# ScalarE's tanh in another order, and the 24-point transforms of later batches spread over four groups

## The chip, the cores and the metric

The kernel runs on one core of one Trainium2 chip. The metric is the device time of one execution in microseconds (us). Shorter is better. Engines are named TensorE (PE in the profile), VectorE (DVE), ScalarE (ACT), GpSimd (POOL) and SyncE (SP, which here only issues DMAs).

## The reference

Three parts follow each other on 24,576 tokens of 256 values (8 batches of 3072), all in float32:

```python
X = np.fft.fft(x, axis=1); X = np.fft.fft(X, axis=2); x = X.real      # part 1, x: (8, 3072, 256)
h = x @ w_in; x = (h - np.tanh(h)) @ w_out                            # part 2, w_in 256x2048, w_out 2048x256
logits = x @ w_gate                                                   # part 3, 8 experts
e = argmax(logits); g = softmax(logits)[e]
out[token] = g * (np.maximum(x @ w1[e], 0) @ w2[e])                   # w1 256x1024, w2 1024x256
```

## The kernel before

Phase 1 computes parts 1 and 2 and the gate for one group of 1024 tokens after the other: 24 groups g, three to a batch (c = g mod 3: first, second and third pass of a batch), and one short pass at the end. The token axis is transformed as 24 x 128: 24-point transforms on VectorE and GpSimd, ahead of time and a batch at once, and a 128-point stage as matmuls at the start of the group before the one that uses it (`dft`, tile `dps`). The transform along the 256 values is folded into w_in.

A group takes 18 steps f. At step f, `uv` makes two products U and V of feature tile f on TensorE (six matmuls of 512 columns: high times high, high times low, low times high part), VectorE reads U into `us` (line 414) and forms h = us - v and us + v (423, 424), one tile for each half of the tokens (s = 0, 1). `tanh` takes each h twice on ScalarE: `t`, in full float32 (432), and `hi`, rounded (433). One step later `split_lo` forms the low part lo = t - hi (440), on GpSimd for s = 0 and on VectorE for s = 1, and `tmm` multiplies hi (eight matmuls, 452) and lo (four, 456) of the step before with w_out into four accumulators. Steps 16 and 17 form the linear part of the output instead of a tanh. All engines work in the order in which the code is written.

In the same steps the gate of the group before is computed: logits (f2, f3), the maximum and softmax (f4 to f6), places within the experts (f7, `place`; its last instruction, line 545, turns them into whole numbers). From f8 to f15 GpSimd writes one column of rows a step to DRAM: a copy of gate and token (576) and an indirect DMA (568), the scatter.

The 24-point transform of a later batch nb is cut into single instructions by `fft_tasks`. Its first 24 steps, each one TENSOR_TENSOR of 128x768 on line 242, go to GpSimd (for batch 1 some to VectorE); the rest, on line 256, go to VectorE. `when` lists the steps of phase 1 that carry them. GpSimd has one of them in each of 24 steps of the third pass of batch nb - 2 (f0 to f14, then from f17 on) and in the first pass of batch nb - 1. VectorE has its part in steps 8 to 15 of that first pass and in 3 to 6 and 8 to 15 of the second. Each comes behind the step's other work on its engine. `load_x` brings the batch from DRAM, issued four steps before the first of them. Two buffers take turns: ya and yb.

Phase 2 is the experts' products. The change does not touch it. The lines on which the sums rest are these, in the order of one step:

```python
hl = [split_lo(th[0], G), split_lo(th[1], V)]     # G: GpSimd, V: VectorE
...
tmm(f - 1, hl)                                    # TensorE, behind the step's U and V
...
th = tanh(hs) if f < KF else None                 # ScalarE
```

Of the kernel before, what the change touches and what calls it, by code (L numbers as in the profile page):

```python
# [10 lines left out]
F32R = mybir.dt.float32r  # L11
# [15 lines left out]
# a row in DRAM: the low halves of its values, their high halves, gate and token, filled up  # L27
ROW = 272
# The rows of an expert come in a first block of 256, then in blocks of 512 and 256. With rows beyond
# the first 256 in pieces of 256, there are 88 to 95 pieces, and at least 40 pairs of one expert.  # L30
# [8 lines left out]
# 24-point classes: (k1 mod 8, k1 mod 3) -> k1; the other classes are mirror images  # L39
# [3 lines left out]
# row of a batch's buffer that holds the real and the sine part of class kb  # L43
# [11 lines left out]
def when(nb):  # L55
    """the steps of phase 1 that carry batch nb's transform: 24 on Pool, the others on DVE"""
    if nb == 1:
        steps = [t for t in range(12, 32) if t != 18]
        return [steps[i * 19 // 24] for i in range(24)], [32, 33, 34, *range(37, 41), *range(42, 50)]
    s = NSTEP * (NCH * nb - 4)  # L60
    return ([s + i + 2 * (i > 14) for i in range(24)],
            [t for t in range(s + 26, s + 52) if t % NSTEP not in (0, 1, 2, 7, 16, 17)])


def parts(kb, ka):
    """slots of a batch's buffer that hold the real and the sine part of class (kb, ka)"""
    if kb in (0, 4):
        return (ROWR[kb], 2 if ka else 0), ((ROWJ[kb], 1) if ka else None)
    return (ROWR[kb], ka), (ROWJ[kb], ka)
# [10 lines left out]
def shape_constants():  # L80
# [17 lines left out]
    # direct and mirrored columns (rows) to even and odd half (columns), for two columns at a time  # L98
# [6 lines left out]
    c96 = np.zeros((2, 2, 24, 32, 2, 2))                     # column, mirror, n1, slot, half, column  # L105
# [37 lines left out]
def layout_inputs(x, w_in, w_out, w_gate, w1, w2):  # L143
    n1 = np.array([[(8 * a + 3 * b) % 24 for a in range(3)] for b in range(8)])
    x4 = x.reshape(B, 24, P, D)[:, n1]                       # batch, b, a, n2, d
    mir = np.zeros((B, 8, 3, P, P), np.float32)
    mir[..., 1:] = x4[..., :P:-1]
    xh = np.concatenate([x4[..., :P], mir], -1)              # batch, b, a, n2, col
    xh = xh.transpose(0, 3, 1, 2, 4)                         # batch, n2, b, a, col
    # batch 0: (column, mirror, n1), column, n2  # L150
# [5 lines left out]
    xz = x[:, :, P].reshape(2, 96, P).transpose(1, 0, 2)     # (4 batches, n1), half, n2  # L156
# [17 lines left out]
def phase1(tc, a, bk, zscr, zny, base, small, ngrp=NGRP):  # L174
# [13 lines left out]
    def bank(shape, name):  # L188
        """the next of the PSUM banks for short use"""
        pool, tag = free_banks.pop(0)  # L190
        free_banks.append((pool, tag))
        return pool.tile(shape, F32, tag=tag, name=name)

    # ---- what stays for the whole phase
# [4 lines left out]
    # high and low parts of w_out, each in two halves; other data have the second one's place at first  # L199
# [20 lines left out]
    def wout(i, f, n=1):  # L220
        """the high or the low part of n f tiles of w_out"""
# [9 lines left out]
    def fft_tasks(y, v, tmp, eng):  # L231
        """24-point transform over the (b, a) slots of y as a list of steps, each some sizes and closures: the slots become
        the classes' real and sine parts, the sine parts of the even half (columns of j and
        256 - j added) with the other sign. eng names the engine of a step, tmp its scratch."""
# [50 lines left out]
        d13 = (y[:, 5], y[:, 7])  # L285
        t5 = tmp(5)
# [3 lines left out]
        two(4, t[:, 0], t[:, 1], pm_ops[::-1], (d13, d13))  # L290
        # R1, R3 = d0 +- c p ; J1, J3 = c q +- d2
# [3 lines left out]
        three(5, 7, False)  # L295
        three(2, 3, True)
        three(0, 1, False)
        three(4, 6, False)
        return out

    def dft_block(ps, y, blk, o, half, m0, m1):
        """one block of 128 slots of the last stage: half 0 from the even, 1 from the odd part"""
# [15 lines left out]
    # ================= groups of 1024 tokens  # L318
# [11 lines left out]
    def dft(g, half):  # L330
        """last stage of the transform for a group; returns what takes it from PSUM"""
# [13 lines left out]
    def nyq(b):  # L345
        """the token of k = N/2, which has no sine part, of batch b"""
# [9 lines left out]
    def nyq_u(f0, f1):  # L356
        """all batches' tokens of k = N/2 up to the tanh, in parts"""
# [22 lines left out]
    def nyq_t():  # L380
        """their products with w_out, a token per partition"""
# [35 lines left out]
    def combine(g, f, us, v):  # L417
        """U and V into the two signs of the token pair"""
# [8 lines left out]
    def tanh(hs):  # L427
        out = []
        for s in range(2):
            t = hp.tile([P, 512], F32, tag="t", name=f"t{s}")  # L430
            hi = sp.tile([P, 512], F32R, tag="hi", name=f"hi{s}")
            S.activation(t, hs[s], AF.Tanh)  # L432
            S.activation(hi, hs[s], AF.Tanh)  # L433
            out.append((t, hi))
# [33 lines left out]
    def logits():  # L468
        # four column groups of the array work side by side
# [22 lines left out]
    # p tokens in each of n columns  # L492
# [9 lines left out]
    def gate2(p=P, n=8, twin=False):  # L502
# [7 lines left out]
        if twin:                         # token 0 is its own partner: counted once  # L510
            V.memset(oh[0:1, 4], 0.0)
# [11 lines left out]
    def rank(p=P, n=8):  # L523
        """places within the experts before the column's token, and in the last column the sums"""
# [9 lines left out]
    def place(p=P, n=8, twin=False):  # L534
# [10 lines left out]
        V.tensor_copy(pi, pf)  # L545
# [5 lines left out]
    def rowT(t, last):  # L551
        """the halves of a column of tokens go through a DMA transpose, the tensor engine has enough to do"""
        s, q = divmod(t, 4)
        if last:                         # the transform's buffer has room for all rows
# [776 lines left out]
```

## Time and profile before

| what | us |
|---|---|
| median of three runs | 3143.38 |
| lowest and highest | 3142.76 and 3144.77 |
| span of the profiled execution | 3140.0 |
| TensorE busy in it | 3038.6 (97%) |
| VectorE busy | 2420.2 (77%) |
| ScalarE busy | 1636.2 (52%) |
| GpSimd busy | 1437.9 (46%) |

The profiled execution's own time is its span, 3140.0 us from the first to the last instruction, 3.4 us under the median of the timed runs. TensorE's granted clock is 0.989 of full speed over the span and 1.00 in the group passes shown below, but for group 2 with 0.93. A busy VectorE or GpSimd also counts time in which an instruction has begun and cannot go on; the mean duration of an instruction is to be compared with that of the same instruction left alone. In the timelines a duration is the instruction's own, and what stands in square brackets is the idle time of the engine ahead of it and what ended it.

### The profile page before, as it was taken

Reading aid. Unit: us, or ns where it says so; the run is one execution under the profiler, and the core shown is the slowest. Engines: PE = TensorE matmul, PEld = TensorE weight load, DVE = VectorE, ACT = ScalarE, POOL = GpSimd, SP = SyncE. Lnnn points to the kernel's source line nnn. Section 1 sums busy time; section 2 is a strip of 40 time slices with the busy share of each in tenths; the row PEclk is TensorE's granted clock in tenths of the full one; section 3 lists DMA queues with packets and bytes.
Section 4 is the critical chain, followed back from the end, with each engine's and each line's share of the span. In section 5 each row is a group of like instructions: output and inputs, shape, how many; then the busy total and the mean of one; then the engine's idle time right before and its main releaser. Section 6 shows DMA issues by size and latency. Waiting matters only on the chain.

```text
span 3140.0 us, 44984 instructions
## 1 busy us (share of the span) xinstructions
PE 3038.6 (97%) x15660; PEld 2485.2 (79%) x15660; DVE 2420.2 (77%) x3998; ACT 1636.2 (52%) x3142; POOL 1437.9 (46%) x1299
## 2 busy tenths in 40 slices
PE   7998999999999999999999999799999999999998
PEld 7775787787787787777788887688888888888886
DVE  7789888888888888888887666676676766767664
ACT  5453455555555555455455555455555555555553
POOL 4566646746746746746744444622222222222222
PEclk9999999999999999999999999899999999999999
DMA  5220112112112112112111111665555556655551
GB/s 180 78 72 23 27 34 69 32 34 69 32 34 70 32 33 71 29 35 72 28 35 35 35 35 32 189 170 155 176 163 155 153 153 176 163 155 154 157 156 40
DMA packets 301615, 278.05 MB, mean 89 GB/s; under 512 B 246046, under 2 KB 261446, under 8 KB 285894
## 3 DMA queue, kind: packets, MB, share of 16 engines
q1 hardware_dynamic: 282422, 222.08, 26.5%
q0 software_dynamic: 18848, 52.99, 4.8%
q8 instruction: 125, 2.05, 0.3%
q14 instruction: 108, 0.88, 0.1%
q10 hardware_dynamic: 112, 0.05, 0.0%
HBM read 168.28 MB, written 55.39 MB: 71 GB/s over the span
## 4 chain that ended last, share of the span: by engine, by line
PE 70%; DVE 12%; issue 5%; ACT 5%; DMA 1%; POOL 0%; DVEq 0%; POOLq 0%; ACTq 0%; SPq 0%
PE acc L452 14%; PE dn L1244 12%; PE acc L456 7%; PE dn L1246 6%; PE up L1231 6%; PE up L1233 6%; PE up L1232 6%; DVE h L423 3%; PE dps L313 2%; ACT hi L433 2%; ACT t L432 2%; DVE us L414 2%; PE u L406 2%; PE u L404 2%; PE u L405 2%
## 5 line engine op out<-in xcount | busy, mean ns | idle before, releaser
L432 ACT ACTIVATE t<-h 128x512 f32<-128x512 f32 x768 | 479.4, 624 | 880.7 <-DVE h L423 880.7
L440 POOL TENSOR_TENSOR lo<-t,hi 128x512 fp32r<-128x512 f32 x384 | 514.0, 1338 | 708.6 <-ACT hi L433 475.1
L1255 POOL DMA_INDIRECT out_dram<-y,i x200 | 235.2, 1176 | 849.2 <-DVE y L1251 341.5
L1244 PE MATMUL dn<-w2s,hh 128*128 128x512 f32 x1600 | 573.0, 398 | 0.0
L414 DVE SCALAR_TENSOR_TENSOR us<-zb,A,u 128x512 f32<-128x512 f32 x432 | 321.3, 744 | 250.0 <-PE u L406 244.1
L433 ACT ACTIVATE hi<-h 128x512 fp32r<-128x512 f32 x768 | 472.8, 616 | 0.0
L1246 PE MATMUL dn<-w2s,hl 128*128 128x256 f32 x1600 | 449.4, 281 | 0.0
L440 DVE TENSOR_TENSOR lo<-t,hi 128x512 fp32r<-128x512 f32 x384 | 392.8, 1023 | 32.6 <-ACT hi L433 28.7
L1244 PEld LDWEIGHTS dn<-w2s,hh 128*128 128x128 f32 x1600 | 301.3, 188 | 69.7
L1231 PE MATMUL up<-xh,w1h 128*128 128x512 f32 (+1 forms) x960 | 344.5, 359 | 9.7 <-ACT xh L1219 9.0
L1232 PE MATMUL up<-xl,w1h 128*128 128x512 f32 (+1 forms) x960 | 341.6, 356 | 1.3 <-DVE xl L1220 1.1
L1233 PE MATMUL up<-xh,w1l 128*128 128x512 f32 (+1 forms) x960 | 342.5, 357 | 0.0
L1251 DVE SCALAR_TENSOR_TENSOR y<-dn,gi,y 128x256 f32<-128x256 f32 x200 | 96.7, 483 | 302.2 <-ACT y L1250 302.1
L1250 ACT ACTIVATE y<-dn,gi 128x256 f32<-128x256 f32 x200 | 95.2, 476 | 423.1 <-PE dn L1246 419.0
L1246 PEld LDWEIGHTS dn<-w2s,hl 128*128 128x128 f32 x1600 | 302.6, 189 | 4.9
L1236 DVE SCALAR_TENSOR_TENSOR hl<-up,hh 128x512 fp32r<-128x512 f32 (+1 forms) x480 | 272.3, 595 | 33.8 <-ACT hh L1235 33.8
L1235 ACT ACTIVATE hh<-up 128x512 fp32r<-128x512 f32 (+1 forms) x480 | 239.0, 521 | 94.6 <-PE up L1233 94.1
L452 PE MATMUL acc<-hi,W0b 128*128 128x512 f32 x768 | 261.8, 405 | 17.5 <-ACT hi L433 15.0
L452 PE MATMUL acc<-hi,W0a 128*128 128x512 f32 x768 | 256.3, 407 | 7.3 <-ACT hi L433 6.8
L423 DVE TENSOR_TENSOR h<-us,v 128x512 f32<-128x512 f32 x384 | 259.7, 676 | 2.6 <-PE v L409 0.2
L424 DVE TENSOR_TENSOR h<-us,v 128x512 f32<-128x512 f32 x384 | 259.6, 676 | 0.0
L452 PE MATMUL acc<-hi,W1b 128*128 128x512 f32 x768 | 238.8, 392 | 0.0
(273 smaller groups left out, 6336.5 us busy)
## 6 DMA issues: line engine op xcount, KB each, us to landing
w<-in_w SPq DMA_DIRECT2D x120, 1024.0 KB
yb<-in_x SPq DMA_DIRECT2D x16, 768.0 KB
ya<-in_x SPq DMA_DIRECT2D x12, 768.0 KB
zb<-zscr SPq DMA_DIRECT2D x24, 256.0 KB
raw<-in_win SPq DMA_DIRECT2D x8, 512.0 KB
raw<-in_wout SPq DMA_DIRECT2D x8, 512.0 KB
out_dram<-y,i POOLq DMA_INDIRECT x200, 4.0
row<-pl SPq DMA_TRANSPOSE x184
```

The lines of the kernel that those rows point to most:

```text
L414: V.scalar_tensor_tensor(us, zb[g], A128[:, f:f + 1], u, ALU.mult, ALU.add)
L423: V.tensor_tensor(hs[0], us, v, ALU.subtract)
L432: S.activation(t, hs[s], AF.Tanh)
L433: S.activation(hi, hs[s], AF.Tanh)
L440: e.tensor_tensor(lo, t, hi.bitcast(F32), ALU.subtract)
L452: T.matmul(acc[i, s], wout(wi, f)[:, c], hl[s][0], start=f == 0 and wi == 0, stop=False)
L1231: T.matmul(ps, w1h[:, k, c], xh[:, k], start=k == 0, stop=False)
L1232: T.matmul(ps, w1h[:, k, c], xl[:, k], start=False, stop=False)
L1233: T.matmul(ps, w1l[:, k, c], xh[:, k], start=False, stop=k == 1)
L1236: V.scalar_tensor_tensor(hl[:, m], ps, 0.0, hh[:, m].bitcast(F32), ALU.max, ALU.subtract)
L1244: T.matmul(ps.rearrange("p a d -> p (a d)"), hh[:, m, c], w2s[:, m].rearrange("p a d -> p (a d)"), start=m == 0, stop=False)
L1246: T.matmul(ps[:, 1], hl[:, m, c], w2s[:, m, 0], start=False, stop=m == 7)
```

## The change

Line numbers of the changed kernel are higher by 25 or so. `tanh` now issues both rounded tanh first and then both full ones. `when` gives GpSimd's steps of batches 2 to 7 other places: four passes instead of two, from step 6 of the second pass of batch nb - 2 on, in steps 0 (two), 1 to 7, 16 and 17 (two) of each pass, and none in 8 to 15. The load is issued at step 1 of that second pass, where it stood at step 14 before. In `fft_tasks`, `first=4` puts one pair of instructions ahead of three others and changes the order of the 3-point parts. The first two of the instructions of each 3-point part of these batches go to GpSimd (they were on VectorE), 48 in all. VectorE's part is spread over steps 1 to 17 of the first and 0 to 16 of the second pass of batch nb - 1. Batch 1 keeps its engines. In `place` the cast goes to GpSimd.

```diff
 def when(nb):
     if nb == 1:
         steps = [t for t in range(12, 32) if t != 18]
-        return [steps[i * 19 // 24] for i in range(24)], [32, 33, 34, *range(37, 41), *range(42, 50)]
-    s = NSTEP * (NCH * nb - 4)
-    return ([s + i + 2 * (i > 14) for i in range(24)],
-            [t for t in range(s + 26, s + 52) if t % NSTEP not in (0, 1, 2, 7, 16, 17)])
+        cut = [[32, 33], [33, 34], [37, 38, 39], [40, 42, 43], [44, 45, 46], [47, 48, 49]]
+        return 8, [steps[i * 19 // 24] for i in range(24)], [(None, c) for c in cut]
+    s = NSTEP * (NCH * nb - 5)
+    slots = [NSTEP * g + t for g in range(4) for t in (0, 0, 1, 2, 3, 4, 5, 6, 7, 16, 17, 17)]
+    slots = [s + t for t in slots if t >= (18 if nb == 2 else 6)]
+    two, rest = slots[:18], slots[18:]
+    r = two[-1] + 1
+    first = [r + 5, r + 10]
+    six = [t for t in rest if t > r + 6][:6]
+    q = max(six[-1], r + 16) + 1
+    end = s + 4 * NSTEP - 1
+    half = (q + end) // 2
+    return s + 1, two + six, [(None, [r, r + 1]), (None, [r + 2, r + 3]),
+                              (first[0], range(first[0] + 1, first[1])),
+                              (first[1], range(first[1] + 1, q)),
+                              (q, range(q + 1, half)), (half, range(half + 1, end))]
@@ fft_tasks
+        if first == 4:
+            two4()
         t5 = tmp(5)
...
-        two(4, t[:, 0], t[:, 1], pm_ops[::-1], (d13, d13))
+        if first != 4:
+            two4()
...
         three(5, 7, False)
+        three(4, 6, False)
         three(2, 3, True)
         three(0, 1, False)
-        three(4, 6, False)
@@ tanh
+        his = []
+        for s in range(2):
+            his.append(sp.tile([P, 512], F32R, tag="hi", name=f"hi{s}"))
+            S.activation(his[s], hs[s], AF.Tanh)
         for s in range(2):
             t = hp.tile([P, 512], F32, tag="t", name=f"t{s}")
-            hi = sp.tile([P, 512], F32R, tag="hi", name=f"hi{s}")
             S.activation(t, hs[s], AF.Tanh)
-            S.activation(hi, hs[s], AF.Tanh)
-            out.append((t, hi))
+            out.append((t, his[s]))
@@ place
-        V.tensor_copy(pi, pf)
+        G.tensor_copy(pi, pf)
@@ the loop over steps
-                if nb * NCH < ngrp and now == when(nb)[0][0] - 4:
+                if nb * NCH < ngrp and now == when(nb)[0]:
                     load_x(nb)
                     fft = fft_tasks(ys[nb], vv, lambda i: tt,
-                                    lambda i, k, nb=nb: V if i == 9 or nb == 1 and (i < 4 and k == 0 or i in (6, 7)) else G)
+                                    lambda i, k, nb=nb: V if nb == 1 and (i == 9 or i < 4 and k == 0 or i in (6, 7)) else G,
+                                    4 if nb > 1 else 5)
...
+                        if at is not None:
+                            fq.setdefault(at, []).extend(fn for _, fn in steps[:2])
+                            steps = steps[2:]
```

ScalarE, one step of group 5, before (full t, then rounded hi, for the one half and then the other), and with the softmax behind it:

```order
L432 ACTIVATE t_5116<-h_5112 128x512
L433 ACTIVATE hi_5117<-h_5112 128x512
L432 ACTIVATE t_5120<-h_5113 128x512
L433 ACTIVATE hi_5121<-h_5113 128x512
L499 ACTIVATE gx<-gd 128x64
```

and after:

```order
L454 ACTIVATE hi_5122<-h_5118 128x512
L454 ACTIVATE hi_5124<-h_5119 128x512
L458 ACTIVATE t_5126<-h_5118 128x512
L458 ACTIVATE t_5128<-h_5119 128x512
L524 ACTIVATE gx<-gd 128x64
```

The high part of the second half has moved up by two places, the full tanh of the first half down by two.

GpSimd in the third pass of a batch (group 8), steps 8 to 10, before: the low part, the copy (576) and scatter (568) of a column of rows, a transform instruction (242) a step.

```order
L440 TENSOR_TENSOR lo<-t_7675,hi_7676 128x512
L576 COPY row_7607<-ggi 128x16
L568 DMA bk<-row_7607,gpi 196608x272
L242 TENSOR_TENSOR tt<-ya 128x768
L440 TENSOR_TENSOR lo<-t_7726,hi_7727 128x512
L576 COPY row_7656<-ggi 128x16
L568 DMA bk<-row_7656,gpi 196608x272
L242 TENSOR_TENSOR tt<-ya 128x768
L440 TENSOR_TENSOR lo<-t_7771,hi_7772 128x512
L576 COPY row_7707<-ggi 128x16
L568 DMA bk<-row_7707,gpi 196608x272
L242 TENSOR_TENSOR ya<-tt 128x2x3x128
```

After, from the low part of step 7 on, with the cast of the positions (570), the copies (601) and the scatters (593):

```order
L465 TENSOR_TENSOR lo<-t_7636,hi_7632 128x512
L570 CAST gpi<-gpf 128x8
L259 TENSOR_TENSOR tt<-ya 128x768
L465 TENSOR_TENSOR lo<-t_7685,hi_7681 128x512
L601 COPY row_7613<-ggi 128x16
L593 DMA bk<-row_7613,gpi 196608x272
L465 TENSOR_TENSOR lo<-t_7736,hi_7732 128x512
L601 COPY row_7662<-ggi 128x16
L593 DMA bk<-row_7662,gpi 196608x272
L465 TENSOR_TENSOR lo<-t_7780,hi_7776 128x512
L601 COPY row_7713<-ggi 128x16
L593 DMA bk<-row_7713,gpi 196608x272
```

The transform instructions (now 259) are gone from behind the scatters; the one of step 7 stands behind the cast.

GpSimd from step 15 to step 1 at the border of a first and a second pass (groups 6 and 7, batch buffer yb), with the engines whose semaphores each waits for, before:

```order
L576 COPY row_6323<-ggi 128x16 [waits DMASW4_49]
L568 DMA bk<-row_6323,gpi 196608x272 [waits DMAHW0_49,Pool_49]
L440 TENSOR_TENSOR lo<-t_6427,hi_6428 128x512 [waits PE_49,Activation_49]
L440 TENSOR_TENSOR lo<-t_6497,hi_6498 128x512 [waits PE_49,Activation_49]
L440 TENSOR_TENSOR lo<-t_6569,hi_6570 128x512 [waits PE_49,Activation_49,Pool_49]
```

and after:

```order
L593 DMA bk<-row_6330,gpi 196608x272 [waits DMAHW0_49,Pool_49]
L465 TENSOR_TENSOR lo<-t_6434,hi_6430 128x512 [waits PE_49,Activation_49]
L259 TENSOR_TENSOR tt<-yb 128x768 x2
L259 TENSOR_TENSOR yb<-yb 128x768 [waits Pool_49] x2
L259 TENSOR_TENSOR yb<-tt 128x768 [waits Pool_49]
L465 TENSOR_TENSOR lo<-t_6507,hi_6503 128x512 [waits PE_49,Activation_49]
L259 TENSOR_TENSOR yb<-tt 128x768 [waits Pool_49]
```

Before, nothing stood between the low parts there. Five transform instructions stand there now, between the low part of step 16 and that of step 1, and one more behind the latter; three of the five wait for one before them on GpSimd itself.

## Rows read from the trace of the kernel before

**Rows 1.** The table of stretches: us, then busy us (instructions) of each engine, clock, DMA.

```profile
812.85:889.22 76.37, 75.23 (x376) 60.49 (x375) 63.96 (x107) 40.85 (x76) 47.22 (x40) 1.00 0.14 33
889.22:966.16 76.94, 76.01 (x377) 60.23 (x376) 69.62 (x125) 40.84 (x76) 36.23 (x33) 1.00 0.26 73
966.16:1048.55 82.39, 79.42 (x379) 59.74 (x377) 66.46 (x93) 40.88 (x77) 63.98 (x48) 1.00 0.14 30
1747.83:1821.61 73.78, 73.78 (x377) 60.79 (x375) 51.64 (x92) 40.85 (x76) 32.42 (x32) 1.00 0.13 34
1821.61:1895.33 73.72, 73.72 (x376) 60.80 (x375) 51.55 (x94) 40.85 (x76) 32.38 (x32) 1.00 0.13 34
237.49:341.37 103.88, 85.66 (x378) 64.26 (x378) 96.76 (x136) 41.16 (x77) 65.53 (x48) 0.93 0.10 24
```

**Rows 2.** The timeline of one step of group 21: start us, us, engine, line, what.

```profile
1795.55 0.39 PE L404 MATMUL u<-pqh,Mh 128*128 128x512 f32 x1
...
1795.63 1.30 POOL L440 TENSOR_TENSOR lo<-t,hi 128x512 fp32r<-128x512 f32 x1 [1.06 <-ACT hi L433]
...
1797.09 0.69 DVE L440 TENSOR_TENSOR lo<-t,hi 128x512 fp32r<-128x512 f32 x1
...
1797.70 0.68 DVE L423 TENSOR_TENSOR h<-us,v 128x512 f32<-128x512 f32 x1
...
1798.47 0.63 ACT L432 ACTIVATE t<-h 128x512 f32<-128x512 f32 x1 [1.37 <-DVE h L423]
...
1798.72 1.07 PE L456 MATMUL acc<-lo,W0b 128*128 128x512 f32 x4
...
1799.53 0.61 ACT L432 ACTIVATE t<-h 128x512 f32<-128x512 f32 x1
1799.63 0.39 PE L404 MATMUL u<-pqh,Mh 128*128 128x512 f32 x1
...
1799.71 1.30 POOL L440 TENSOR_TENSOR lo<-t,hi 128x512 fp32r<-128x512 f32 x1 [1.06 <-ACT hi L433]
```

**Rows 3.** The timeline in group 9, steps 4 and 5, where low parts meet.

```profile
832.07 1.29 POOL L440 TENSOR_TENSOR lo<-t,hi 128x512 fp32r<-128x512 f32 x1 [2.52 <-issue]
...
833.08 0.84 DVE L440 TENSOR_TENSOR lo<-t,hi 128x512 fp32r<-128x512 f32 x1
...
833.32 2.31 POOL L242 TENSOR_TENSOR ya<-tt 128x768 f32<-128x768 f32 x1
...
837.14 1.85 POOL L242 TENSOR_TENSOR ya<-tt 128x768 f32<-128x768 f32 x1
837.20 2.34 DVE L440 TENSOR_TENSOR lo<-t,hi 128x512 fp32r<-128x512 f32 x1
```

**Rows 4.** The timeline in group 11, a third pass, step 11.

```profile
1017.00 0.63 ACT L432 ACTIVATE t<-h 128x512 f32<-128x512 f32 x1 [2.31 <-DVE h L423]
...
1017.67 1.84 POOL L242 TENSOR_TENSOR yb<-tt 128x768 f32<-128x768 f32 x1
...
1019.23 2.08 DVE L440 TENSOR_TENSOR lo<-t,hi 128x512 fp32r<-128x512 f32 x1 [0.40 <-ACT hi L433]
...
1019.47 1.29 POOL L440 TENSOR_TENSOR lo<-t,hi 128x512 fp32r<-128x512 f32 x1
...
1022.00 0.64 ACT L432 ACTIVATE t<-h 128x512 f32<-128x512 f32 x1 [2.28 <-DVE h L423]
```

**Rows 5.** The timeline in group 2, a transform instruction on VectorE.

```profile
293.69 3.62 DVE L256 TENSOR_TENSOR yb<-yb 128x256 f32<-128x256 f32 x1
...
293.92 1.86 POOL L242 TENSOR_TENSOR tt<-ya 128x768 f32<-128x768 f32 x1
...
295.73 1.30 POOL L440 TENSOR_TENSOR lo<-t,hi 128x512 fp32r<-128x512 f32 x1
```

**Rows 6.** Groups of instructions by line: xcount, busy us, mean ns, idle before.

```profile
L545 DVE CAST gpi<-gpf 128x8 int32<-128x8 f32 (+1 forms) x25 | 23.5, 941 | 6.0 <-DVE gpf L542 3.8 <-DVE gpf L544 2.2
```

**Rows 7.** The timeline of the DMA queue of SP around a load.

```profile
951.14 3.92 SPq L229 DMA_DIRECT2D yb<-in_x  x4
```

More of the change, by code (lines that the diff above doesn't have):

```diff
@@ L229, in load_x, with fft_tasks @@
             Q.dma_start(y[:, i:i + 5:4], a["x"][b - 1][:, i:i + 5:4])
-    def fft_tasks(y, v, tmp, eng):
+    def fft_tasks(y, v, tmp, eng, first=4):
         w = y.shape[-1]
@@ L285, in fft_tasks, with two4 @@
         d13 = (y[:, 5], y[:, 7])
+        def two4():
+            two(4, t[:, 0], t[:, 1], pm_ops[::-1], (d13, d13))
+        if first == 4:
+            two4()
         t5 = tmp(5)
@@ L1021, in phase1 @@
             for nb in range(1, B):
-                if nb * NCH < ngrp and now == when(nb)[0][0] - 4:
+                if nb * NCH < ngrp and now == when(nb)[0]:
                     load_x(nb)
                     fft = fft_tasks(ys[nb], vv, lambda i: tt,
-                                    lambda i, k, nb=nb: V if i == 9 or nb == 1 and (i < 4 and k == 0 or i in (6, 7)) else G)
-                    pool, dve = when(nb)
+                                    lambda i, k, nb=nb: V if nb == 1 and (i == 9 or i < 4 and k == 0 or i in (6, 7)) else G,
+                                    4 if nb > 1 else 5)
+                    _, pool, parts_at = when(nb)
                     for t, part in zip(pool, fft):
                         fq.setdefault(t, []).append(part[0][1])
-                    steps = [x for part in fft[24:] for x in part]
-                    size = sum(n for n, _ in steps)
-                    done = 0
-                    for n, fn in steps:
-                        fq.setdefault(dve[done * len(dve) // size], []).append(fn)
-                        done += n
+                    rest_of = fft[24:]
+                    cuts = [rest_of[:1], rest_of[1:2], rest_of[2:6], rest_of[6:10], rest_of[10:13], rest_of[13:]]
+                    for (at, dve), part in zip(parts_at, cuts):
+                        steps = [x for p in part for x in p]
+                        if at is not None:
+                            fq.setdefault(at, []).extend(fn for _, fn in steps[:2])
+                            steps = steps[2:]
+                        size = sum(n for n, _ in steps)
+                        done = 0
+                        for n, fn in steps:
+                            fq.setdefault(dve[done * len(dve) // size], []).append(fn)
+                            done += n
             for fn in fq.pop(now, ()):
```

## The prediction

> **What bounds the kernel now.** I first read the table of stretches, with the borders of the group passes put in, to see which passes are longer than their TensorE work [rows 1]. The reader is to see that a pass without any transform work takes 73.78 or 73.72 us and is TensorE from end to end (PE busy 73.78 and 73.72), while the three passes of a batch take 76.37, 76.94 and 82.39. I call the floor 73.75. The excess over it is 2.6, 3.2 and 8.6 us, 14.45 a batch, which is what the change can win back there. The pass of group 2 stands alone with 103.88. Phase 2 is not touched.
>
> Second, the timeline of one undisturbed step [rows 2], which gives the step's loop. TensorE starts the step at S = 1795.55 and the next at 1799.63: 4.08 us. VectorE's low part ends at 1797.78, the first h at 1798.38, .60 later, and ScalarE starts its four tanh, one each 0.53 us, at A = 1798.47, S + 2.92. GpSimd's low part of that tanh starts at 1799.71, A + 1.24, after the second tanh. VectorE's low part begins at 1797.09, S + 1.54, when GpSimd's (1795.63 to 1796.93) is over. So in a clean step the two do not meet.
>
> Third, the timelines of steps where they do meet. In [rows 3] VectorE's low part starts (833.08) while GpSimd's runs (to 833.36) and ends at 833.92, 0.56 after it; 111 low parts of VectorE began so, and each ended 0.55 after GpSimd's, while one left alone takes 0.69 [rows 2]. A transform instruction holds it the same way: 837.14 to 838.99 on GpSimd, VectorE done at 839.54 [rows 3]. In the last pass of a batch the chain closes on this [rows 4]: a transform instruction starts at 1017.67, runs 1.84 us, GpSimd's next low part follows at once and VectorE's waits for both (1019.23, 2.08 us), so that ScalarE, which began at 1017.00, begins again at 1022.00: steps of 5.0 instead of 4.08. That is what the change takes apart.
>
> **The change part by part.** *The order of the tanh.* GpSimd's low part waits for the full tanh of the first half, now third. The third starts at A + 1.06 (1799.53) and runs 0.61 [rows 2]; with the 0.08 us that now lie between the end of the second and GpSimd's start, it begins at A + 1.75 and with 1.30 us ends at A + 3.05. VectorE's needs the fourth, as before, and is asked for at S + 1.54 of the next step, A + 2.70: now GpSimd's is still running. By [rows 3] it then ends 0.56 behind it, at A + 3.61, the first h 0.60 later, ScalarE 0.09 after that: A + 4.30. The loop from tanh to tanh was covered by the 4.08 us of TensorE; it now takes 4.30 and sets the step, 0.22 late each time. There is slack: TensorE wants the second low part at 1798.95 (the second matmul of the four that start at 1798.72), S + 3.40 and so A + 4.56 by the step before, about 0.9 us after it is there. Steps f0, f2, f3 and f6 carry more TensorE work and give slack back; nine steps f7 to f15 use 9 x 0.22 = 2.0, of which 0.9 is covered, so 1.1, and in f16, where TensorE has only twelve matmuls, the late low part and the h behind it show at about their full 1.2. Together 2.3 us for every pass from group 1 on, transform or not. Bounds: 0 if the loop hides, 3.5 if no slack helps (16 x 0.22).
>
> The Trainium skill ("SBUF — State Buffer", section "Who interferes with whom") says that a VectorE instruction with two SBUF inputs contends with a GpSimd instruction that reads SBUF, and that issue order decides which one blocks. The trace agrees (111 of 111), and by that rule the new order hurts VectorE in every step.
>
> *The twenty-four transform steps on GpSimd.* In the last pass of a batch f8 to f14 lose theirs: 4.08 instead of 5.0. In f1 to f7 there is still one a step, but VectorE's low part now stands waiting behind GpSimd's and goes ahead of the transform instruction, as in [rows 3], where the transform (833.32, 2.31 us) waits for it. What is left: five transform instructions between the low parts of f16 and f1, 5 x 1.85 = 9.25 us. Any two-input VectorE instruction there waits for one or more; the first two passes have such ones at f16, f17, f0 and f1. A wait costs between 0.6 (the end of one instruction) and 9.25 (all five); [rows 5] shows one that let two GpSimd instructions pass (3.62 us). I take 2.7 us at the border of the first to the second pass and 1.4 at that of the second to the third, where only short ones stand.
>
> *The cast of the positions* leaves VectorE, where it takes 0.94 on average, 25 times, mostly waiting [rows 6], and is now in GpSimd's queue at f7, waiting for VectorE's last gate instruction. In the second and third pass a transform instruction is queued behind it (1.85), and behind that the next low part, which starts about 1.6 late. The first pass has nothing behind it. Bounds 0 and 2.1.
>
> *Forty-eight two-input instructions go to GpSimd*, two at a time, four times a batch. Those behind a scatter (f11 of the first pass, f9 of the second) hold GpSimd for about 1.2 us each (two thirds of 1.85), so its low part is 1.2 late; those at f6 and f2 lie in steps with slack. The Trainium skill ("GPSIMD Engine Reference", section "4.1 Engine selection") advises VectorE for two-input work, GpSimd being about half as fast; the low parts agree, 1.30 against 0.69.
>
> *The load of the next batch* is issued thirteen steps earlier on SP, ahead of the row transposes. A load's issues took 3.92 us of the queue [rows 7], and five steps, over 20 us, now lie before its first use: nothing.
>
> *The sum* over the six later batches, against the excess now. First pass: 2.3 + 1.2 + 0.2 = 3.7 for 2.6, six times, +6.6. Second: 2.3 + 1.6 + 1.2 + 2.7 = 7.8 for 3.2, six times and less 1.6 where the last batch has no successor, +26. Third: 2.3 + 1.6 + 1.4 = 5.3 for 8.6, five times, -16.5. Group 2 loses seven transform instructions between f8 and f14 that VectorE, which is busy 96.76 of its 103.88 us there [rows 1], had to wait out [rows 5]: 7 x 1.85 = -13, with bounds -20 and 0. Groups 0 and 1: +4. Groups 20 to 23, clean until now: 4 x 2.3, +9.2. In all +16.3: a span of 3156.3. The median is 3.4 us above the profiled span of 3140.0, so 3159.7, and I say 3160.
>
> **The rivals.** *The new order costs nothing*: the two low parts meet but TensorE's steps still cover the loop, for instance because the high parts, both there by A + 1.2, let TensorE's order of work absorb it. Then 23 x 2.3 = 53 us fall away: 3107, faster. For it: the slack of 0.9, the long steps, and that TensorE waited for ScalarE's high part in loaded steps. Against it: the sum above has 0.22 left over in each of nine steps in a row, and no pair of the 111 overlapped. Chance 0.27.
>
> *VectorE slips in between the transform instructions* at the borders: their self-waits leave gaps. The terms 2.7 and 1.4 go, 6 x 2.7 + 5 x 1.4 = 23: 3137. For it: GpSimd's low part lets VectorE in [rows 3]. Against: [rows 4] and [rows 5], where the instruction behind a transform instruction went ahead of the waiting VectorE. Chance 0.17.
>
> *VectorE is shut out for the whole run*: a two-input instruction at f16 waits for all five, and the us and h behind it, so TensorE stands. Each border then costs about 5 us more, 11 x 5 = 55: 3215. It decides if GpSimd keeps its place from one transform instruction to the next as it does for a low part [rows 4]. Against: most of the five wait for their predecessor, which should open the place. Chance 0.14.
>
> That steps f8 to f14 stay at 5.0 because the scatter alone makes them so is ruled out by the first pass, which scatters in these steps and takes 76.37 in all.
>
> **How the numbers follow.** Forecast 0.42, rivals 0.27, 0.17 and 0.14. The forecast's own range is 3145 to 3180. What a measurement of this kernel can tell from no change is about 0.2%, 6.3 us. Faster by more: the first rival and some of the second, 0.34. Within: the rest of the second and the lower edge of the forecast, 0.16. Slower: 0.50. The range 3090 to 3200 takes in the first two rivals and leaves out most of the last.
>
> **What would show it.** In the profile after, group passes 20 to 22 tell the first step apart from all others: 76 us if the loop is right, 73.8 if not, with VectorE's low parts at 0.9 rather than 0.69 there. Third passes should fall from 82.4 to 79, with f8 to f15 no longer at 5.0; second passes should rise from 76.9 to about 81.5, the loss at f7, f9 and between f16 and f1; group 2 should be near 91. If clean passes stay at 73.8 the forecast is wrong, and if second passes stay under 78 its second half is.

## The result, and the profile after

The changed kernel takes 3167.21 us (median; 3166.03 to 3168.73), the kernel before, timed beside it, 3143.07. The ratio is 1.008 with a 95% interval of 1.0066 to 1.0095: slower by 0.8%. The forecast was 3160, in a range of 3090 to 3200. The profiled span grew from 3140.0 to 3164.2 us, by 24.2.

The table of stretches of the changed kernel, one line for each group pass shown in [rows 1] (the second clean one left out): us, then busy us (instructions) of PE, PEld, DVE, ACT and POOL, clock, DMA share, GB/s.

```profile
811.47:889.57 78.10, 76.09 (x377) 60.32 (x376) 67.77 (x110) 42.49 (x76) 47.34 (x42) 1.00 0.13 32
889.57:971.87 82.30, 77.30 (x377) 61.10 (x375) 66.78 (x110) 42.30 (x76) 55.47 (x47) 0.98 0.22 69
971.87:1051.50 79.63, 76.97 (x378) 60.40 (x378) 63.59 (x93) 42.61 (x77) 56.27 (x45) 1.00 0.12 32
1765.21:1842.20 76.99, 76.37 (x377) 60.16 (x375) 60.14 (x91) 42.48 (x76) 33.55 (x33) 1.00 0.12 33
244.29:332.49 88.20, 79.97 (x378) 59.69 (x377) 81.84 (x135) 42.78 (x77) 53.02 (x43) 1.00 0.11 29
```

The lines stand for group 9 (first pass, 76.37 before), group 10 (second, 76.94), group 11 (third, 82.39), group 21 (clean, 73.78) and group 2 (103.88). Over all groups, by the first matmul of each: first passes +14.2 us in sum, second +24.3, third -15.2, group 2 -15.7, groups 0 and 1 +6.6, groups 20 to 22 +9.5. These make 23.7 of the 24.2. The rest of the kernel, from group 23 on, grew by 0.3: group 23 by 3.3, as the other clean passes did, while the stretch behind it to the end was 3.0 shorter, which the prediction did not expect.

Group 10 is the longest of the six second passes (80.1 to 82.3). In its step f2, 6.73 us where the other five take 5.33 to 5.37, TensorE's granted clock was half for 3 us, which is its level of 1.2 instead of 2.4 GHz; just before, TensorE had waited 1.91 us for VectorE's low part.

```profile
901.00:904.00 3.00, 3.00 (x15) 1.90 (x17) 2.08 (x5) 1.95 (x4) 1.50 (x2) 0.50 1.02 409
```

A clean step of group 21, to be held against [rows 2]. Start us, us, engine, line, what. ScalarE first (two of a kind are in one row):

```profile
1808.85 1.29 ACT L454 ACTIVATE hi<-h 128x512 fp32r<-128x512 f32 x2 [1.52 <-DVE h L446]
1810.05 1.14 ACT L458 ACTIVATE t<-h 128x512 f32<-128x512 f32 x2
...
1813.22 1.29 ACT L454 ACTIVATE hi<-h 128x512 fp32r<-128x512 f32 x2 [1.52 <-DVE h L446]
```

GpSimd's low part waits for the first of the full tanh:

```profile
1810.75 1.29 POOL L465 TENSOR_TENSOR lo<-t,hi 128x512 fp32r<-128x512 f32 x1 [1.21 <-ACT t L458]
...
1815.12 1.28 POOL L465 TENSOR_TENSOR lo<-t,hi 128x512 fp32r<-128x512 f32 x1 [1.20 <-ACT t L458]
```

VectorE's waits for the second, and then takes 1.37 us instead of 0.69:

```profile
1811.21 1.37 DVE L465 TENSOR_TENSOR lo<-t,hi 128x512 fp32r<-128x512 f32 x1 [0.48 <-ACT t L458]
1812.51 0.68 DVE L446 TENSOR_TENSOR h<-us,v 128x512 f32<-128x512 f32 x1
```

and TensorE, whose four matmuls of the low parts run 1.31 us where they ran 1.07:

```profile
1809.09 0.40 PE L427 MATMUL u<-pqh,Mh 128*128 128x512 f32 x1
...
1812.31 1.31 PE L481 MATMUL acc<-lo,W0b 128*128 128x512 f32 x4
1813.46 0.40 PE L427 MATMUL u<-pqh,Mh 128*128 128x512 f32 x1
```

From A = 1808.85: GpSimd's low part begins at 1810.75, A + 1.90, and ends at A + 3.19. VectorE's, asked for at 1811.21 while it runs, ends at 1812.58, 0.54 behind it, at A + 3.73; ScalarE begins again at 1813.22, A + 4.37. This is the loop of the prediction, and the step is now 4.37 us long (TensorE's from 1809.09 to 1813.46). By line:

```profile
L465 POOL TENSOR_TENSOR lo<-t,hi 128x512 fp32r<-128x512 f32 x384 | 509.5, 1327 | 604.5 <-ACT t L458 486.3 <-issue 73.4 <-PE u L429 16.5
...
L465 DVE TENSOR_TENSOR lo<-t,hi 128x512 fp32r<-128x512 f32 x384 | 468.2, 1219 | 63.7 <-ACT t L458 61.3
...
L570 POOL CAST gpi<-gpf 128x8 int32<-128x8 f32 (+1 forms) x25 | 7.5, 299 | 76.7 <-DVE gpf L567 34.9 <-DVE gpf L569 21.6 <-ACT hi L454 15.2
```

The kernel before:

```profile
L440 DVE TENSOR_TENSOR lo<-t,hi 128x512 fp32r<-128x512 f32 x384 | 392.8, 1023 | 32.6 <-ACT hi L433 28.7
```

VectorE's low parts take 1219 ns on average, where they took 1023; the cast takes 299 ns on GpSimd, where VectorE needed 941 [rows 6].

### The profile page after: what moved, and what is told of

The parts are those of the page before. It is cut to its first block, busy times and chain, and to the rows that moved or that the text cites. A ratio compares the mean times of both kernels' runs of the same rounds, so it can differ in the third digit from the quotient of the medians.

```text
span 3164.2 us, 44463 instructions
## 1 busy us (share of the span) xinstructions
PE 3041.3 (96%) x15660; PEld 2485.4 (79%) x15660; DVE 2434.9 (77%) x3925; ACT 1674.5 (53%) x3142; POOL 1508.9 (48%) x1372
## 5 line engine op out<-in xcount | busy, mean ns | idle before, releaser
L454 ACT ACTIVATE hi<-h 128x512 fp32r<-128x512 f32 x768 | 483.2, 632 | 869.1 <-DVE h L446 860.5
L465 DVE TENSOR_TENSOR lo<-t,hi 128x512 fp32r<-128x512 f32 x384 | 468.2, 1219 | 63.7 <-ACT t L458 61.3
L458 ACT ACTIVATE t<-h 128x512 f32<-128x512 f32 x768 | 436.4, 616 | 0.0
L481 PE MATMUL acc<-lo,W0b 128*128 128x512 f32 x768 | 241.3, 413 | 30.0 <-POOL lo L465 28.2
L481 PE MATMUL acc<-lo,W0a 128*128 128x512 f32 x768 | 219.9, 400 | 38.3 <-POOL lo L465 20.0
L477 PE MATMUL acc<-hi,W0a 128*128 128x512 f32 x768 | 245.1, 400 | 0.2
```

Of the source, the lines that this page charges most:

```text
L454: S.activation(his[s], hs[s], AF.Tanh)
L465: e.tensor_tensor(lo, t, hi.bitcast(F32), ALU.subtract)
L477: T.matmul(acc[i, s], wout(wi, f)[:, c], hl[s][0], start=f == 0 and wi == 0, stop=False)
L481: T.matmul(acc[i, s], wout(0, f)[:, c], hl[s][1], start=False, stop=f == KF - 1)
```

## The experiments

Each kernel was timed 4 to 11 times beside the kernel before, whose median there lay between 3140.2 and 3143.1; the ratio is to that, so ratios of different rows compare better than medians. The table gives the length of one group pass of each kind (groups 9, 10, 11, a clean one, 21, and group 2), from the first matmul of a group to that of the next in the profile, and the median and ratio of the timed runs. "Exchanged" means that VectorE takes the low part of the first half, ahead of us, and GpSimd that of the second.

| kernel | first | second | third | clean | group 2 | median us | ratio (95%) |
|---|---|---|---|---|---|---|---|
| before | 76.4 | 76.9 | 82.4 | 73.8 | 103.9 | 3143.07 | |
| changed | 78.1 | 82.3 | 79.6 | 77.0 | 88.2 | 3167.21 | 1.008 (1.0066 to 1.0095) |
| changed, old tanh order | 76.0 | 78.7 | 77.2 | 73.6 | 89.9 | 3112.59 | 0.9909 (0.9893 to 0.9924) |
| before, new tanh order | 77.0 | 77.5 | 81.5 | 77.0 | 101.5 | 3163.05 | 1.0063 (1.0049 to 1.0077) |
| changed, hi t hi t | 75.6 | 78.6 | 78.3 | 73.7 | 89.8 | 3118.66 | 0.9929 (0.9915 to 0.9942) |
| changed, cast on VectorE | 78.3 | 82.5 | 80.1 | 77.0 | 88.3 | 3168.05 | 1.0082 (1.0068 to 1.0096) |
| old order, exchanged | 73.9 | 78.4 | 75.5 | 73.4 | 88.3 | 3084.35 | 0.9822 (0.9809 to 0.9836) |
| before, exchanged | 74.4 | 73.4 | 82.3 | 73.4 | 103.8 | 3104.79 | 0.9885 (0.987 to 0.99) |
| old order, 48 on VectorE | 76.0 | 77.8 | 77.2 | 73.6 | 89.7 | 3108.12 | 0.9896 (0.9881 to 0.9912) |
| old order, one a step in f1 to f8 | 75.9 | 84.8 | 77.1 | 73.7 | 90.4 | 3137.60 | 0.9989 (0.998 to 0.9998) |
| changed, exchanged | 74.0 | 80.8 | 75.9 | 73.4 | 88.8 | 3098.33 | 0.987 (0.9855 to 0.9885) |
| first attempt at a best version | 74.4 | 86.2 | 88.2 | 73.4 | 87.9 | 3213.73 | 1.0231 (1.0217 to 1.0245) |
| second attempt | 76.3 | 80.2 | 75.5 | 73.4 | 88.2 | 3102.16 | 0.9871 (0.9855 to 0.9888) |
| old order, exchanged, 48 on VectorE | 74.1 | 79.0 | 75.5 | 73.4 | 87.9 | 3080.90 | 0.9806 (0.9792 to 0.9819) |

**The old order of the tanh in the changed kernel.** The full tanh of a half is issued ahead of its rounded one again, and both halves in turn:

```diff
-            his.append(sp.tile([P, 512], F32R, tag="hi", name=f"hi{s}"))
-            S.activation(his[s], hs[s], AF.Tanh)
...
             S.activation(t, hs[s], AF.Tanh)
+            S.activation(hi, hs[s], AF.Tanh)
```

> The changed kernel with the old order of the tanh (t, hi, t, hi); the spread transform stays. Theory (the late low part on GpSimd closes a loop of 4.3 us in every step): passes without transform work go from 76.99 back to 73.75 us and VectorE's low part there from 1.36 to 0.69; the passes of a batch gain less, 1 to 3 us each, since VectorE's low part again starts ahead of GpSimd's and is shut out by a transform instruction behind it. 4 x 3.2 and 18 x 2: some 50 us less, 3110 to 3130, faster than the kernel before. Rival (the loss in clean passes comes from the cast on GpSimd or the scatters, the order is free): no change, 3160 to 3170.

Measured 3112.59, some 54 us less than with the new order, in the range of the theory. Clean passes are back at 73.64. The change without its new order (the spread, with the cast and the 48 instructions on GpSimd; "the spread" from here on) is therefore 0.9% faster than the kernel before: what made the change slower is the order of the tanh.

**The new order alone in the kernel before** (the reverse of that edit, in the other kernel).

> The kernel before with nothing but the new order of the tanh. Theory: clean passes 77.0 instead of 73.75 (4 of them, +13); in the first and second passes steps f5 to f9 lose their 4.7 (VectorE's low part now goes ahead of the transform instruction), and clean steps gain 0.3 each, about even; third passes keep 5.0 in f10 to f15, since GpSimd alone is busy 4.9 us in them. In all 3150 to 3165. Rival (rounded parts first help TensorE in loaded steps more than the loop costs): below 3140.

Measured 3163.05, inside the theory's numbers and far from the rival's. First passes take what clean ones take, 77.0: with this order a transform instruction in f0 to f7 costs nothing more, since VectorE's low part waits behind GpSimd's and goes ahead of the transform instruction (in 86 of the 86 places of this run where one follows GpSimd's low part at once), and the loop costs 3.2 in its place.

The two edits do not add. The order alone costs some 20 us, the spread alone gains some 29 (ratios 1.0063 and 0.9909 of 3140.16), together they would give -9; measured is +25 (1.008). In the old order the spread took 5.2 us from a third pass (82.4 to 77.2), in the new one 1.9 (81.5 to 79.6). By steps of group 11, the 2.5 us between the two orders of the spread lie above all at f8 (5.9 instead of 4.9), f0 (5.7 instead of 5.0) and f3 and f4 (0.7 together), and only 0.6 at f13 to f15, where the loop sets the step. So it is mostly where GpSimd has other work that the late low part costs more.

**A third order, hi t hi t.**

```diff
-            his.append(sp.tile([P, 512], F32R, tag="hi", name=f"hi{s}"))
-            S.activation(his[s], hs[s], AF.Tanh)
...
+            S.activation(hi, hs[s], AF.Tanh)
             S.activation(t, hs[s], AF.Tanh)
```

> The changed kernel with a third order of the tanh: hi, t, hi, t. GpSimd's low part has its operands as early as in the old order (end of the second tanh), the second rounded part comes third (A + 1.06 to A + 1.68) instead of last. Theory (only the start of GpSimd's low part counts): as with the old order within 5 us, clean passes 73.8, 3110 to 3130. Rival (what counts is when the second rounded part is there): between the old order and the changed kernel, clean passes near 75.5.

Measured 3118.66, 6 us over the old order, one more than the theory allowed; clean passes 73.67. So in a clean pass it is the start of GpSimd's low part that counts, and when the second rounded part is there does not matter. Most of the 6 us are in the five third passes, 78.3 instead of 77.2; why is open.

**The cast back on VectorE** (`V.tensor_copy(pi, pf)` in `place`).

> The changed kernel with the cast of the positions back on VectorE. Theory (the cast makes GpSimd wait at f7, and the transform instruction behind it then delays the next low part): f8 of second and third passes, now 5.7 to 6.0 us, falls to about 4.4 to 4.7, 11 x 1.3 = 14 us less: 3150. Rival (the transform instruction alone makes f8 long): no change at f8, 3160 to 3170.

Measured 3168.05: no gain, though the step it was about did what the theory said. GpSimd at steps 7 and 8 of group 10, changed kernel:

```profile
925.78 1.30 POOL L465 TENSOR_TENSOR lo<-t,hi 128x512 fp32r<-128x512 f32 x1 [0.86 <-POOL tt L259]
929.78 0.19 POOL L570 CAST gpi<-gpf 128x8 int32<-128x8 f32 x1 [2.71 <-DVE gpf L569]
929.94 1.84 POOL L259 TENSOR_TENSOR tt<-yb 128x768 f32<-128x768 f32 x1
931.74 1.73 POOL L465 TENSOR_TENSOR lo<-t,hi 128x512 fp32r<-128x512 f32 x1
```

and with the cast on VectorE, where the transform instruction (926.23) no longer waits for the gate:

```profile
924.97 1.30 POOL L465 TENSOR_TENSOR lo<-t,hi 128x512 fp32r<-128x512 f32 x1 [0.86 <-POOL tt L259]
926.23 2.31 POOL L259 TENSOR_TENSOR tt<-yb 128x768 f32<-128x768 f32 x1
929.40 1.43 POOL L465 TENSOR_TENSOR lo<-t,hi 128x512 fp32r<-128x512 f32 x1 [0.86 <-POOL tt L259]
...
933.91 1.29 POOL L465 TENSOR_TENSOR lo<-t,hi 128x512 fp32r<-128x512 f32 x1 [1.20 <-ACT t L458]
```

Step f8 fell from 5.77 to 4.26 us (first matmul to first matmul) in this pass, but f9 grew from 4.10 to 4.38 and f10, with the pair of 3-point instructions, from 4.62 to 5.94. In group 5 f8 fell from 5.92 to 4.41 and f9 to f13 grew from 4.08 to 4.26 up to 4.38 each, so that of 1.5 us some 1.3 came back. In both passes the steps behind a long one run at 4.08 for a while, and without the long one at 4.36 to 4.38: the time saved at f8 is spent in the steps that follow.

The same step shows how VectorE and GpSimd take turns. In the changed kernel VectorE's low part begins while the transform instruction runs, ends 0.54 us behind it, and it is GpSimd's low part (931.74, 1.73 us instead of 1.29) that stands:

```profile
930.62 1.70 DVE L465 TENSOR_TENSOR lo<-t,hi 128x512 fp32r<-128x512 f32 x1
```

**The low parts exchanged.**

```diff
                 u, v = uv(g, f)
+            if th is not None:
+                hl = [split_lo(th[0], V), split_lo(th[1], G)]
+            if not last:
                 us = take_u(g, f, u)
...
-            if th is not None:
-                hl = [split_lo(th[0], G), split_lo(th[1], V)]
```

With the old order and the spread:

> The changed kernel with the old order of the tanh, and the two low parts exchanged: VectorE takes the first half's, ahead of us, GpSimd the second half's. Theory (all of the loss is VectorE's low part held by a GpSimd instruction that started before): VectorE's starts at A + 1.25, when GpSimd has finished or not begun, and GpSimd's runs from A + 2.3 to A + 3.6, beside us and h, which read PSUM; TensorE needs it at A + 4.56. So ScalarE starts at about S + 2.3 instead of S + 2.92, clean passes stay at 73.75, VectorE's low parts average 0.7, and the passes of a batch, 76.0, 78.7 and 77.2 with the old order alone, fall by 1 to 3 us each: 3060 to 3090. Rival (what is lost is the time of the transform instructions on GpSimd themselves): 3105 to 3120.

Measured 3084.35, in the theory's range. A clean step: ScalarE,

```profile
1739.51 0.63 ACT L455 ACTIVATE t<-h 128x512 f32<-128x512 f32 x1 [1.37 <-DVE h L446]
```

VectorE,

```profile
1740.70 0.69 DVE L463 TENSOR_TENSOR lo<-t,hi 128x512 fp32r<-128x512 f32 x1 [0.68 <-ACT hi L456]
1741.96 0.75 DVE L437 SCALAR_TENSOR_TENSOR us<-zb,A,u 128x512 f32<-128x512 f32 x1 [0.57 <-PE u L429]
```

and GpSimd:

```profile
1737.72 1.29 POOL L463 TENSOR_TENSOR lo<-t,hi 128x512 fp32r<-128x512 f32 x1 [1.39 <-ACT hi L456]
...
1741.80 1.29 POOL L463 TENSOR_TENSOR lo<-t,hi 128x512 fp32r<-128x512 f32 x1 [1.38 <-ACT hi L456]
```

VectorE's low part lies from A + 1.19 to A + 1.88 and GpSimd's from A + 2.29 to A + 3.58, and us stands beside the latter without being held. In the kernel before:

> The kernel before with the low parts exchanged in the same way and its transform where it was. Theory: steps f5 to f9 of first and second passes (4.5 to 4.7) fall to 4.1 to 4.3; third passes keep 5.0 in f10 to f15 if GpSimd's own work of 4.9 us there sets them, and fall to 4.8 or less if the wait on VectorE did. 18 passes by 1 to 2 us and group 2 by some 8: 3100 to 3120. Rival (no gain from the exchange): 3135 to 3145.

Measured 3104.79, in the range. First and second passes lose nearly all their excess (74.4 and 73.4); group 2, which was to gain some 8, gains nothing (103.8), and the third passes keep theirs. There a transform instruction stands behind a scatter in each step, and VectorE's low part, though it begins first, is held for more than 1 us in 18 of the 20 places of this run where it begins during such a scatter. One of them in group 11, VectorE and then GpSimd:

```profile
1000.38 3.73 DVE L440 TENSOR_TENSOR lo<-t,hi 128x512 fp32r<-128x512 f32 x1 [0.68 <-ACT hi L433]
```

```profile
999.43 1.00 POOL L568 DMA_INDIRECT bk<-row,gpi  x1 [0.28 <-PE acc L452]
1000.47 1.84 POOL L242 TENSOR_TENSOR yb<-tt 128x768 f32<-128x768 f32 x1
1002.27 1.28 POOL L440 TENSOR_TENSOR lo<-t,hi 128x512 fp32r<-128x512 f32 x1
```

And in the changed kernel, whose new order of the tanh is kept:

> The changed kernel, its new order of the tanh kept, with only the low parts exchanged (VectorE the first half's, ahead of us; GpSimd the second half's). Theory (the new order hurts only because it moves the two low parts onto each other): VectorE's starts at A + 1.75 and ends before GpSimd's begins at A + 2.3, clean passes 73.4 to 73.8, as with the old order and the exchange within 8 us: 3080 to 3092. Rival (the late full parts cost something of their own): 3110 or more.

Measured 3098.33, 6 us over the range, but 69 under the changed kernel. Clean passes are at 73.43, so the order costs them nothing once the low parts do not meet. The range was missed since the new order still costs 14 us against the old one with the exchange, elsewhere: 5 in group 1, and 5 in second passes, above all where a pair of 3-point instructions lies behind a scatter (f10 5.6 against 4.6 with the old order); the rest is spread. What the late full parts do there was not followed up.

**The 48 instructions of the 3-point parts back on VectorE**, with the old order (`V if i == 9` for all batches):

> The changed kernel with the old order of the tanh and the 48 instructions of the 3-point parts back on VectorE. Theory (behind a scatter they make GpSimd's low part late): f12 of first passes from 4.54 to 4.1 and f10 of second passes from 4.95 to 4.1; VectorE's own work in these steps grows by 1 us, which it has room for. 6 x 1.3 = 8 us less than with the old order alone: 3105. Rival (VectorE has no room, or waits there): 3112 or more.

Measured 3108.12, 4 us under the old order alone, with intervals that overlap. By steps, f12 of first passes fell from 4.54 to 4.08 and f10 of second passes from 4.95 to 4.08; f8 and f9 of first ones, where VectorE now does this work, took 0.6 and 0.3 more.

**No run of five at the border** (slots `range(1, 9)` for batches 3 to 7, old order):

> The changed kernel with the old order of the tanh and, for batches 3 to 7, GpSimd's 24 steps one at a time in f1 to f8 of each pass: none between the low parts of f16 and f1; VectorE's part lies in f8 to f17 of the first and f1 to f16 of the second pass. Theory (the run of five at the border costs a step f16 of 4.1 instead of 2.73 in every pass, and f1 of the second pass 1.6): 5 x (3 x 1.38 + 1.6 + 0.2) = 30 us less than with the old order alone, less some 5 for a transform instruction behind the scatter of f8: 3085 to 3095. Rival (f16 is long for another reason): 3110 or more.

Measured 3137.60, 25 us worse than the old order alone. What the theory said of the border came true: f16 fell from 4.11 to 2.73 in every pass, f1 of second passes from 5.75 to 4.21. The time came back at f8 of second passes, 9.0 to 9.8 us in four of the six where it was 5.1: a pair of 3-point instructions, the cast, two transform instructions and a scatter now meet in f7 and f8.

**Attempts at a best version.** The first one, for batches 3 to 7:

```diff
+    if nb > 2:
+        slots = [11, 13, 15, 17, *(18 + t for t in (*range(8), 9, 11, 13, 15, 17)), *range(36, 43)]
+        return s + 3, [s + t for t in slots], [(None, [...])]
```

The 3-point instructions of these batches are on VectorE again, too.

> A version put together from what the runs showed: old order of the tanh, low parts exchanged, and for batches 3 to 7 GpSimd's transform instructions one a step in f0 to f7 and every second step (9, 11, 13, 15, 17) beside the scatters, from f11 of the second pass on, done by f6 of the first; VectorE's part as in the kernel before, batch 2 as in the changed kernel. Theory (a low part on VectorE that starts first is free, and GpSimd's work per step must stay under 4.08 us on average): third passes 74 to 75 instead of 82.4, first and second ones 73.5 to 75, group 2 about 88: some 40 less than the exchange alone gave in the kernel before, 3055 to 3070. Rival (a transform instruction behind a scatter makes a step long even if the next has none): third passes 77 to 79, 3085.

In this kernel one pair of the transform is overwritten in its scratch tile before it is used, so the values of batches 3 to 7, and with them phase 2, are others; only its group passes can be read. They refute the theory, and the rival's 77 to 79 as well: third passes took 88.2 in group 11. VectorE in step 16 of group 11:

```profile
1047.80 4.05 DVE L466 TENSOR_TENSOR lo<-t,hi 128x512 fp32r<-128x512 f32 x1 [0.68 <-ACT hi L459]
```

and GpSimd beside it:

```profile
1047.18 0.99 POOL L594 DMA_INDIRECT bk<-row,gpi  x1 [0.28 <-POOL row L602]
1048.19 1.86 POOL L262 TENSOR_TENSOR yb<-tt 128x768 f32<-128x768 f32 x1
1049.98 1.31 POOL L466 TENSOR_TENSOR lo<-t,hi 128x512 fp32r<-128x512 f32 x1
1051.22 0.69 POOL L602 COPY row<-ggi 128x16 f32<-128x16 f32 x1
```

VectorE's low part begins 0.39 us ahead of the transform instruction, but while a scatter runs. It ends at 1051.85, 0.56 behind the end of GpSimd's low part (1051.29): it has let the transform instruction and the low part pass, but not the copy, which ends at 1051.91. The second attempt put none behind a scatter:

> A version put together from what the runs showed: old order of the tanh, low parts exchanged, the 3-point parts' instructions on VectorE, and for batches 3 to 7 GpSimd's transform instructions one a step in f0 to f7 and f17 of each pass, none behind a scatter; so two, not five, between the low parts of f16 and f1. Theory (what is left of the loss with the exchange is the run at the border, f17 3.8, f0 5.7, f1 6.4, and the pairs behind scatters, f10 and f12 4.5): 5 x 4 us less for the borders and 6 x 1 for the pairs than the exchange with the spread as it was: 3055 to 3065. Rival (spreading to more steps only moves the waits): 3080 to 3090.

Measured 3102.16, above both ranges, and 18 us worse than the exchange with the spread as it was. The rival's reason fits: the long steps are others now. f0 of the second pass of group 10 took 7.3 us and f7 and f8 5.3 and 5.5, and f17 of five first passes 4.6. Last, what had gained alone was put together:

> The best version so far (old order of the tanh, low parts exchanged, transform spread as in the changed kernel) with the 48 instructions of the 3-point parts back on VectorE. Theory (the pairs behind scatters still cost a step of about 4.5 at f10 and f12, and nothing is given back): 6 x 0.9 = 5 us less, 3077 to 3082. Rival (VectorE, now first in each step with its low part, is held longer by its own added work): 3085 or more.

Measured 3080.90, in the theory's range, 1.9% faster than the kernel before and 86 us under the changed kernel: the lowest median found, though its interval overlaps that of the exchange without the 48. The steps f10 and f12 fell to 4.08, but f8 of first passes rose from 4.08 to 4.59.

## Why the prediction was right

**The loop.** Right in its place and its mechanism, a little small: 4.37 us a step where 4.30 was said, and 3.2 us a pass where 2.3 was. GpSimd's low part starts at A + 1.90, not A + 1.75. The step that was missed: the second tanh now reads the second half's h, which ends at A + 0.56 (1809.41), so it starts at A + 0.66 and the third at A + 1.20, where the sum took A + 1.06 from the old order, in which the second tanh reads the first h again. By steps, a clean pass stays at the old lengths to f7 and takes 4.35 to 4.40 from f9 to f15 and 3.88 in f16, which is 1.16 over its length before, as said (1.2); the seven steps give 1.9 where 1.1 was said.

**Third passes.** 79.05 was said (73.75 and 5.3), 79.6 came; the sum over five was -15.2 where -16.5 was said. The 5.0 of f10 to f15 are gone, and 4.08 (to f12) to 4.4 (from f13 on) came in their place. Much of what is left of the loss is at f8 (5.9) and f0 (5.7).

**Second passes.** +24.3 for +26. The terms at the border were about right, but not for the reason given: f1 of the second pass takes 6.4 to 6.5 us instead of 4.17 in five of the six passes, where 2.7 was said for this border, and f17 and the next f0 about 1.9 more in sum, where 1.4 was. Group 9 to 10, GpSimd (two of a kind in one row; they end at 887.83, 889.82, 891.62 and 893.58):

```profile
884.31 1.28 POOL L465 TENSOR_TENSOR lo<-t,hi 128x512 fp32r<-128x512 f32 x1 [1.21 <-ACT t L458]
885.55 4.27 POOL L259 TENSOR_TENSOR tt<-ya 128x768 f32<-128x768 f32 x2
889.79 3.79 POOL L259 TENSOR_TENSOR ya<-ya 128x768 f32<-128x768 f32 x2
893.54 1.84 POOL L259 TENSOR_TENSOR ya<-tt 128x768 f32<-128x768 f32 x1
895.33 1.32 POOL L465 TENSOR_TENSOR lo<-t,hi 128x512 fp32r<-128x512 f32 x1
```

and VectorE:

```profile
887.25 0.86 DVE L273 SCALAR_TENSOR_TENSOR ya<-vv,ya 128x256 f32<-128x256 f32 x1
...
890.08 1.82 DVE L273 SCALAR_TENSOR_TENSOR ya<-vv,ya 128x256 f32<-128x256 f32 x1
891.83 0.73 DVE L437 SCALAR_TENSOR_TENSOR us<-zb,A,u 128x512 f32<-128x512 f32 x1
...
893.87 2.47 DVE L485 TENSOR_TENSOR lin<-lin,acc 128x512 f32<-128x512 f32 x4
896.26 1.28 DVE L364 TENSOR_TENSOR pql<-dps,pqh 128x512 fp32r<-128x512 f32 x2
897.46 1.33 DVE L273 SCALAR_TENSOR_TENSOR ya<-vv,ya 128x128 f32<-128x128 f32 x2
898.71 0.73 DVE L437 SCALAR_TENSOR_TENSOR us<-zb,A,u 128x512 f32<-128x512 f32 x1
```

VectorE does get in behind the transform instruction that holds it: the first two-input instruction (887.25) takes 0.86 and ends 0.28 us behind the transform instruction, the second (890.08) 1.82 and ends 0.28 behind the third of them. [rows 4] and [rows 5], which the prediction weighed against this, both show a transform instruction that begins right behind a scatter (0.03 and 0.02 us), and at the border none does (see the last section). So the mechanism of the second rival is what happens, and its waits are short, but its time (3137) did not come with it. They put us at 891.83, and f0 is a step in which VectorE has over 5 us of work of its own (the sums of the accumulators, 893.87, and the low parts of the next operands, 896.26), so the lateness is handed on with 1.33 more until us of f1 at 898.71. f1 takes 6.54 us.

**First passes.** The term that was mis-sized most: +14.2 for +6.6. Group 3 alone makes 4.3 of the 7.6: 77.45 was said (73.75 and 3.7), 81.7 came. In batch 2 both pairs of 3-point instructions that lie in the first pass stand behind a scatter, and f11 and f16 take 5.95 and 5.87 us; the sum put one of the two into a step with slack. In the others (78.1 to 78.8) the pair makes f12 5.95, 1.9 over 4.08, where 1.2 was said, with 1.31 and 1.29 us for its two instructions on GpSimd; and the long step takes the loop's excess off f13 to f15, which are at 4.08.

**The cast.** 1.6 us a pass was said and shown as a step (f8 5.9), but taking it away gained nothing. The terms of the sum were added as if independent; with a loop over the limit they are not: behind a long step the loop's own excess is gone for some steps. So the sum came out nearer than its terms. The loop alone was too small by 0.9 in each of 23 passes, 21 us, yet +24.2 came where +16.3 was said: first passes came out 7.6 over their term, and the clean ones, groups 0 and 1 and the third passes 1.3 to 2.6 each, but second passes, group 2 and the end of the kernel 1.7 to 2.7 under theirs. That 3160 lies so near 3167 is in part luck.

**Group 2.** -13 was said, -15.7 came; not tested by itself, but the old order with the spread has it too (89.9), and the new order alone does not (101.5).

The rival that the new order costs nothing is refuted by the two runs that move the order alone; that VectorE is shut out for a whole run of transform instructions did not happen at the border, though it did behind a scatter in the first attempt at a best version (last section).

## What to carry to other kernels

When two engines hold each other up, as VectorE and GpSimd do here, work out from one clean step when each starts, for the changed order too; ask of each instruction what it reads there, not only when its engine is free. Then look at the whole loop: one that was 0.3 us over the limit cost that in every step that had no slack left. Here moving an operand's producer by a place or two cost more (54 us within the spread) than the whole new schedule of background work gained (29), and giving the operand that is ready first to VectorE, ahead of its other work, made clean passes no longer (73.4). Losses in such a loop don't add: test the part that moves the loop's length by itself first.

## What the runs showed of the hardware

Whether a waiting VectorE gets its turn behind a GpSimd instruction goes with what stood ahead of that instruction. Take the places where VectorE's low part is under way when a two-input instruction of GpSimd that is no low part (a transform instruction, or at the start one that prepares weights) ends, and GpSimd's next two-input instruction follows at once. Where the former had itself begun right behind a scatter, VectorE let the next one pass as well, 30 of 30 times in the kernel before ([rows 4] is one) and 3 of 3 in the changed kernel. Where it had not, VectorE came next, 3 of 3 and 27 of 27 times (930.62 above). Over all kernels but the first attempt at a best version these are 116 of 116 and 206 of 206.

It is the same for a low part that begins during the scatter and is still running when a transform instruction follows: 4.05 and 3.73 us above for one that takes 0.69 alone, and 7.54 us in another step of the first attempt (from 1057.93), where four instructions of GpSimd in a row went first. Where nothing followed the scatter at once, the low part took its 0.68 us, 20 of 20 times in the kernel before. So a scatter does not hold VectorE by itself; it goes together with GpSimd keeping its place for what comes right behind it. Why is not shown: no run changed the scatter alone.
